# Seven block products for the last tile's second layer, and its weight sums on other engines

## The chip, the cores and the metric

The kernel runs on one core of a Trainium2 chip. The core has five engines that run at the same time and meet only through semaphores: TensorE (PE, matrix products), VectorE (DVE), ScalarE (ACT), GpSimd (POOL) and SyncE (SP, which issues transfers). Matrix products end in PSUM, a memory of eight banks of 128 x 512 fp32; everything else lies in SBUF. PE, DVE and ACT reach PSUM, GpSimd only SBUF.

The metric is the device time of one execution in microseconds (us). The kernel before took a median of 279.95 us in three runs (279.79 to 280.09).

## The reference

A linear attention is followed by a two-layer network. Cut to what is computed:

```python
# q, k, v: (8 batches, 8 heads, 576 rows, 64)
q_s = softmax(q, over the 64)
k_s = softmax(k, over the 576 rows)
kv  = einsum('bhsd,bhse->bhde', k_s, v)
x   = einsum('bhsd,bhde->bhse', q_s, kv)   # becomes 4608 tokens x 512
h   = x @ w_in                             # 512 x 2048
g   = maximum(0.01 * h, h)
out = g @ w_out                            # 2048 x 512
```

## The kernel before

The 4608 tokens are cut into nine tiles of 512 (`NT`, `TT`). A tile's first layer (`layer1`, L562) is 16 blocks j of 128 features, each the sum of four matmuls of 512 columns in bf16; ACT applies the leaky function (`leaky`, L572) and writes bf16 blocks g. The second layer (`layer2`, L584) makes for each of four groups of 128 tokens the sum of 16 matmuls; `store` (L577) copies the bank to SBUF and issues two transfers on SP's queue.

The attention of batch b is spread over the tiles before the one that needs it. The order of all work is written out by hand: `at(t, u, ...)` hangs functions on the point (tile t, step u), and `run(t, u)` calls them when the emission gets there. Steps 0 to 15 are the blocks of the first layer, 16 to 31 quarters of the token groups of the second. Each engine runs its own instructions strictly in the order of emission. `attend` (L486) writes the product of q and kv for some rows into banks, `x_keep` (L495) copies it into x's transposed store `xT`. For the last batch `at(6, 15)` (L817) attends seven of nine rows (`R7`, four banks) and then the last two (`RE`, two banks), the copies shared between ACT and DVE, and calls `token_sums`.

Banks come from two pools: `psB_pool` with six and `psO_pool` with two, the latter for the second layer's sums. The six buffers `raw_pool` hold the raw q, k, v of two batches, 9 KB per partition each, and serve other uses when the last batch has been read.

The last two tiles (TA = 7, TB = 8) do their first layer together, as a 2 x 2 product of blocks (tokens of tile 7 and 8; lower and upper half of the 512 inputs; lower and upper half of the 2048 features). It is done with seven block products in place of eight, by sums of blocks before and after. `weight_sums` (L791, at (6, 2)) makes t1 to t4 for all of w_in on DVE, four subtractions of 2048 elements, and GpSimd copies b22; the five results take five raw buffers. `token_sums` (L801) makes s1 to s4 on DVE and a22 on ACT. Sums and copies are fp32r, a 4-byte type for products. `pair_layer1` (L948) does one of eight row blocks i: seven products (`product`, L934) of two matmuls of 512 columns, with the additions on DVE (L958). Two products are plain bf16 (w_in by x), five are fp32r. Between the products PE does steps from `fill_steps`: the second layer of tile 6 that is left, then `pair_step` (L986), the second layer of tile 7. Tile 7's blocks lie in `g7`, tile 8's in `g8`, both where x of the tiles already used (`spent`) was.

Behind the eighth block PE finishes tile 7's second layer (L992), then does tile 8's (L1036): four groups of 16 matmuls of 512 columns, the last group cut at column 384 so that ACT and DVE copy its two parts.

The strip of code that orders the last attention and the sums:

```python
at(6, 2, weight_sums)
at(6, 15, lambda: attend_all(B - 1, (R7, (nc.scalar, nc.vector)), (RE, (nc.scalar, nc.vector))), token_sums)
```

Of the kernel before, what the change touches and what calls it, by code (L numbers as in the profile page):

```python
# [20 lines left out]
L = 64  # L21
# [5 lines left out]
def kernel(  # L27
# [499 lines left out]
    def attend_rows(b, rows, engs=(nc.scalar, nc.scalar)):  # L527
        groups = ((0, 1),) if rows.stop - rows.start <= 4 else ((0,), (1,))
        for ggs in groups:
            attend(b, ggs, rows)  # L530
# [253 lines left out]

    def plain(n):
# [5 lines left out]
    def weight_sums():  # L791
        w = lambda cs, fh: w_in_sb[:, cs, fh * (F // 2) : (fh + 1) * (F // 2)]
        for n in ("t1", "t3", "t2", "t4", "b22"):
            late[n] = raw_pool.tile([P, 2, R * HL * D // 2], F32R, name=n, tag="raw")[:, :, 0 : F // 2]
        subtract(nc.vector, "t1", w(CL, 1), w(CL, 0))
        subtract(nc.vector, "t2", w(CR, 1), plain("t1"))
        subtract(nc.vector, "t3", w(CR, 1), w(CL, 1))
        subtract(nc.vector, "t4", w(CR, 0), plain("t2"))
        nc.gpsimd.tensor_copy(out=late["b22"], in_=w(CR, 1))

    def token_sums():  # L801
        front.close()
        pool = ctx.enter_context(tc.tile_pool(name="late", bufs=1, reuse_waits="tile"))
        late["pool"] = ctx.enter_context(tc.tile_pool(name="late2", bufs=2, reuse_waits="tile"))
        both = raw_pool.tile([P, 2, R * HL * D // 2], F32R, name="s13", tag="raw")
        for i, n in enumerate(("s1", "s3")):
            late[n] = both[:, i, 0 : 2 * TT].rearrange("p (c n) -> p c n", c=2)
        for n in ("s2", "s4", "a22"):
# [97 lines left out]
    def layer2_at(t, g, tsub):  # L906
        po = psO_pool.tile([P, O], FP32, name="pout", tag="pout")
# [8 lines left out]
    for t in range(1, TA):  # L916
# [8 lines left out]
        for tsub in range(NTS if t < TA - 1 else 1):  # L925
            for _ in layer2_at(t, g_sb, tsub):
# [148 lines left out]
```

## Time and profile before

| | us |
|---|---|
| median of three runs | 279.95 |
| the profiled execution | 280.43 |
| its span, first to last instruction | 278.6 |
| TensorE busy | 270.6 |
| VectorE busy | 213.0 |
| ScalarE busy | 162.5 |
| GpSimd busy | 51.7 |

The times in the profile count from the start of the span. A row of the timeline reads: start, length, engine, line of the kernel, operation, output and inputs by name, shapes, how many instructions are merged into it, and in brackets how long the engine was idle before and what ended that. A row of the groups by form reads: line, engine, operation, names, shape and count, then busy us and mean ns of one, then idle time before. `PEld` is PE's weight load, which can run beside a matmul. The length of one matmul's record is longer than the time until the next can start, since matmuls are pipelined; the pace is read from many of them. A few matmul records can be missing from a trace.

### The profile page before, as it was taken

What the parts mean: (1) busy time and instruction counts of PE and PEld (TensorE: products, weight loads), DVE (VectorE), ACT (ScalarE), POOL (GpSimd) and SP (SyncE); (2) the same over time, 40 slices, a digit from 0 to 9 for tenths busy, and PEclk for the clock granted to TensorE, in tenths of its full rate; (3) what the DMA queues carried; (4) which work ended last, traced back from release to release, by engine and by line L of the source; (5) the groups of instructions that cost most, each with busy time, mean ns of one, the idle gap of its engine ahead of it and who ended that gap; (6) DMA issues with size and microseconds to landing.
All of it is one profiled execution on the core that took longest, in us unless ns stands there. A gap on an engine that the chain in (4) does not pass through costs nothing.

```text
span 278.6 us, 4917 instructions
## 1 busy us (share of the span) xinstructions
PE 270.6 (97%) x1912; PEld 135.7 (49%) x1938; DVE 213.0 (76%) x299; ACT 162.5 (58%) x285; POOL 51.7 (19%) x56
## 2 busy tenths in 40 slices
PE   8799999999999999999999999999999999999994
PEld 3378644444444444444444544454445555554443
DVE  2996985999999949966885597978959999891321
ACT  3977573783488367755586448664673757652000
POOL 2867450259003003000400070020000000000000
PEclk9999999999999999999999999999999999999999
DMA  6999999995994697099309930330601011100183
GB/s 236 341 208 324 242 255 309 396 307 160 287 406 167 91 395 262 2 251 397 100 0 269 390 86 2 85 76 1 161 0 40 0 38 40 38 1 0 43 185 75
DMA packets 40007, 46.46 MB, mean 167 GB/s; under 512 B 18736, under 2 KB 23344, under 8 KB 39984
## 3 DMA queue, kind: packets, MB, share of 16 engines
q1 hardware_dynamic: 36320, 41.82, 48.3%
q0 software_dynamic: 3504, 4.20, 8.7%
q8 instruction: 15, 0.25, 0.3%
q10 hardware_dynamic: 160, 0.13, 0.1%
q14 instruction: 8, 0.07, 0.1%
HBM read 36.70 MB, written 9.44 MB: 166 GB/s over the span
## 4 chain that ended last, share of the span: by engine, by line
PE 92%; DVE 3%; DMA 2%; issue 1%; ACT 0%; SPq 0%
PE pout L585 35%; PE ph L564 35%; PE pp L937 9%; PE pout L992 5%; PE pout L1036 5%; DMA k_raw<-in_k_dram 2%; PE po L478 1%; DVE t L159 1%; PE pokv L340 1%; PE pkv L340 1%; PE pkv L418 0%; DVE k_raw L409 0%; DVE e L958 0%; ACT ke L205 0%; DVE kmax L159 0%
## 5 line engine op out<-in xcount | busy, mean ns | idle before, releaser
L585 PE MATMUL pout<-w_out_sb,gj 128*128 128x512 bf16 x432 | 104.7, 380 | 1.1 <-issue 0.5
L564 PE MATMUL ph<-xT,w_in_sb 128*128 128x512 bf16 (+1 forms) x505 | 98.3, 352 | 0.4
L573 ACT ACTIVATE gj<-ph 128x512 bf16<-128x512 f32 x112 | 63.5, 602 | 19.1 <-PE ph L564 18.1
L564 PEld LDWEIGHTS <-w_in_sb 128*128 128x128 bf16 x512 | 49.8, 98 | 47.0 <-issue 0.2
L585 PEld LDWEIGHTS <-gj 128*128 128x128 bf16 x448 | 42.5, 98 | 54.9 <-issue 8.1
L579 ACT COPY out_sb<-pout 128x512 f32<-128x512 f32 (+1 forms) x25 | 14.5, 579 | 56.2 <-PE pout L1036 21.8
L217 POOL CAST vb<-v_raw 128x1152 bf16<-128x1152 f32 x13 | 21.4, 1680 | 82.7 <-DMA v_raw<-in_v_dram 82.7
L320 DVE TENSOR_REDUCE qsum<-qe 128x36 f32<-128x2304 bf16 (+5 forms) x13 | 20.0, 1542 | 6.9 <-ACT qe L311 6.7
L205 ACT ACTIVATE ke<-k_raw 128x2304 bf16<-128x2304 f32 (+2 forms) x13 | 18.0, 1383 | 7.9 <-DVE k_raw L197 7.7
L958 DVE TENSOR_TENSOR u<-pp,u 128x512 f32<-128x512 f32 x32 | 20.9, 685 | 1.8 <-PE pout L585 0.5
L327 DVE TENSOR_TENSOR qe<-qe,qrec 128x2304 bf16<-128x2304 bf16 (+5 forms) x13 | 21.5, 1657 | 0.5
L579 DVE COPY out_sb<-pout 128x512 f32<-128x512 f32 (+1 forms) x12 | 7.3, 652 | 18.8 <-PE pout L992 8.8
L244 DVE TENSOR_REDUCE qmax<-q_raw 128x36 f32<-128x2304 f32 (+5 forms) x13 | 19.9, 1536 | 0.0
L311 ACT ACTIVATE qe<-q_raw 128x2304 bf16<-128x2304 f32 (+5 forms) x13 | 17.2, 1321 | 3.7 <-POOL q_raw L303 2.8
L937 PE MATMUL pp<-s,t 128*128 128x512 f32 x48 | 18.6, 489 | 0.0
L197 DVE TENSOR_TENSOR k_raw<-k_raw,kall 128x1152 f32<-128x1152 f32 (+2 forms) x10 | 18.0, 1820 | 0.3
L303 POOL TENSOR_TENSOR q_raw<-q_raw,qmax 128x512 f32<-128x512 f32 (+3 forms) x7 | 11.8, 1682 | 20.5 <-DVE qmax L244 19.4
L303 DVE TENSOR_TENSOR q_raw<-q_raw,qmax 128x2304 f32<-128x2304 f32 (+1 forms) x6 | 14.7, 2448 | 0.2
L159 DVE TENSOR_TENSOR t<-t 128x256 f32<-128x256 f32 (+2 forms) x22 | 14.0, 636 | 0.7
L1036 PE MATMUL pout<-w_out_sb,xT 128*128 128x512 bf16 (+2 forms) x79 | 14.0, 336 | 0.1
L501 ACT CAST xT<-po 128x448 bf16<-128x448 f32 (+3 forms) x31 | 13.3, 513 | 1.1 <-PE po L478 1.1
L360 DVE RECIPROCAL krec<-pokv 128x2 f32<-128x2 f32 x8 | 1.3, 163 | 15.3 <-PE pokv L478 15.3
(100 smaller groups left out, 262.1 us busy)
## 6 DMA issues: line engine op xcount, KB each, us to landing
out_dram<-out_sb SPq DMA_DIRECT2D x70, 128.0 KB, 3.4
q_raw<-in_q_dram SPq DMA_DIRECT2D x6, 1152.0 KB, 9.3
v_raw<-in_v_dram SPq DMA_DIRECT2D x6, 1152.0 KB, 12.0
k_raw<-in_k_dram SPq DMA_DIRECT2D x5, 1152.0 KB, 7.3
k_raw<-in_k_dram SPq DMA_DIRECT2D x6, 576.0 KB, 5.7
v_raw<-in_v_dram SPq DMA_DIRECT2D x4, 576.0 KB, 7.7
w_in_sb<-in_moe_w_in_dram POOLq DMA_DIRECT2D x7, 256.0 KB, 6.8
w_out_sb<-in_moe_w_out_dram POOLq DMA_DIRECT2D x6, 256.0 KB, 9.2
```

What stands on the lines that cost most here:

```text
L217: eng.tensor_copy(out=o, in_=i)
L244: nc.vector.tensor_reduce(out=o, in_=st[b]["q"][:, hs, rs], axis=AX.X, op=ALU.max)
L303: eng.tensor_tensor(out=qs, in0=qs, in1=st[b]["qmax", rs.start, hs.start].unsqueeze(3).to_broadcast([P, m, n, D]), op=ALU.subtract,)
L320: nc.vector.reduce_sum(out=qsum, in_=q_cols(b, rs, hs), axis=AX.X)
L327: nc.vector.tensor_tensor(out=qes if out is None else out, in0=qes, in1=st[b]["qrec", rs.start, hs.start].unsqueeze(3).to_broadcast([P, n, ...
L564: nc.tensor.matmul(ph, lhsT=w_in_sb[:, cb, j * P : (j + 1) * P], rhs=xT[:, cb, c0 : c0 + n], start=(cb == 0 and first), stop=(cb == NB - 1 ...
L573: nc.scalar.activation(out=o, in_=ph, func=AF.Prelu, alpha=LEAKY_SLOPE)
L579: copy(out=out_sb, in_=pout)
L585: nc.tensor.matmul(pout, lhsT=g_sb[j // 2][:, j % 2, tsub * P : (tsub + 1) * P], rhs=w_out_sb[:, j, os], start=(j == 0), stop=(j == NF - 1),)
L937: nc.tensor.matmul(ps, lhsT=w(c)[:, i * P : (i + 1) * P], rhs=a(c), start=(c == 0), stop=(c == 1))
L958: nc.vector.tensor_tensor(out=o, in0=ps, in1=e, op=ALU.add)
L1036: nc.tensor.matmul(po, lhsT=g8(j)[:, tsub * P : (tsub + 1) * P], rhs=w_out_sb[:, j, os], start=(j == 0), stop=(j == NF - 1),)
```

## The change

Second layer of tile 8: the product of g (tokens by 2048 features) and w_out (2048 by 512) is now done with seven block products too. Its blocks are the two halves of the 512 tokens, of the 2048 features and of the 512 outputs. `product2` does one: 2 x 8 matmuls of 128 tokens by 256 columns, so 112 matmuls of 256 columns in all. Two products are plain bf16 (32 matmuls), five take fp32r sums (80). `out_weight_sums` makes v1 to v4 from w_out on DVE at (6, 2), and GpSimd copies o22. The sums of g (r1 to r4 on DVE, c22 on ACT) are made behind the last block of the pair stage, in memory that the pair stage's pools give back (`pairs.close()`). The partial results are added on DVE; the first and last output blocks are stored as soon as they are there, one half of each group issued by SP and one by ACT. Tile 7's stores copy on ACT.

w_in's sums: `in_weight_sums(i)` makes t1 to t4 for one row block, four subtractions of 256 elements on GpSimd, into one strip with room for two blocks; blocks 0 and 1 at (5, 26), block i + 2 behind block i. b22 is copied by block too (`last_weights`). In block 0 a copy of c22's first column on GpSimd stands ahead of the sums of block 2.

The last batch's two rows attend into the two banks of `psO_pool`; the first group of tile 6's second layer takes a bank of `psB_pool` instead. u2 and c22 have one buffer each instead of two, s1 and s3 their own tiles.

```diff
-    def attend(b, ggs, rows):
+    def attend(b, ggs, rows, pool=psB_pool, tag=BANK_TAG):
         n = (rows.stop - rows.start) * L
-        ps = [
-            psB_pool.tile([P, len(ggs), n], FP32, name="po", tag=BANK_TAG) for _ in range(2)
-        ]
+        ps = [pool.tile([P, len(ggs), n], FP32, name="po", tag=tag) for _ in range(2)]
...
-    def weight_sums():
-        w = lambda cs, fh: w_in_sb[:, cs, fh * (F // 2) : (fh + 1) * (F // 2)]
...
+    def out_weight_tiles():
+        for n in ("v1", "v3", "v2", "v4", "o22"):
+            late[n] = strip(n).rearrange("p a b -> p (a b)")[:, 0 : NH * H2].rearrange("p (m o) -> p m o", o=H2)
+
+    def out_weight_sums():
+        w = lambda fh, os: w_out_sb[:, fh * NH : (fh + 1) * NH, os]
+        subtract(nc.vector, "v1", w(0, E2), w(0, E1))
+        subtract(nc.vector, "v2", w(1, E2), plain("v1"))
+        subtract(nc.vector, "v3", w(1, E2), w(0, E2))
+        subtract(nc.vector, "v4", w(1, E1), plain("v2"))
+        nc.gpsimd.tensor_copy(out=late["o22"], in_=w(1, E2))
+
+    def in_weight_sums(i):
+        w = lambda cs, fh: w_in_sb[:, cs, (fh * NH + i) * P : (fh * NH + i + 1) * P]
+        if i == 0:
+            late["t"] = strip("t")
+        for n, k in zip(("t1", "t2", "t3", "t4"), range(4)):
+            late[n, i] = late["t"][:, k, i % 2 * 256 : i % 2 * 256 + 256].rearrange("p (c f) -> p c f", c=2)
+        for n, x, y in (
+            ("t1", w(CL, 1), w(CL, 0)),
+            ("t2", w(CR, 1), plain(("t1", i))),
+            ("t3", w(CR, 1), w(CL, 1)),
+            ("t4", w(CR, 0), plain(("t2", i))),
+        ):
+            subtract(nc.gpsimd, (n, i), x, y)
+        if i > 1:
+            last_weights(i)
+
+    def last_weights(i):
+        late["b22", i] = late["pool"].tile([P, 2, P], F32R, name="b22")
+        nc.gpsimd.tensor_copy(out=late["b22", i], in_=w_in_sb[:, CR, (NH + i) * P : (NH + i + 1) * P])
...
-    at(6, 2, weight_sums)
-    at(6, 15, lambda: attend_all(B - 1, (R7, (nc.scalar, nc.vector)), (RE, (nc.scalar, nc.vector))), token_sums)
+        last_weights(0)
+        last_weights(1)
+
+    at(5, 26, out_weight_tiles, lambda: in_weight_sums(0), lambda: in_weight_sums(1))
+    at(6, 2, out_weight_sums)
+    both = (nc.scalar, nc.vector)
+    at(6, 15, lambda: attend_all(B - 1, (R7, both), (RE, both, psO_pool, "pout")), token_sums)
...
-            for _ in layer2_at(t, g_sb, tsub):
+            for _ in layer2_at(t, g_sb, tsub, *((psB_pool, BANK_TAG) if t == TA - 1 else ())):
...
         add(c22, p5, u3)
+        if i == 0:
+            nc.gpsimd.tensor_copy(out=gate, in_=c22[:, 0:1])
...
+        if i + 2 < NH:
+            in_weight_sums(i + 2)
...
+    for first in (True, False):
+        for b in range(2):
...
+            if first:
+                nc.scalar.copy(out=o("c22"), in_=a22)
+                nc.vector.tensor_tensor(out=o("r1"), in0=a21, in1=a22, op=ALU.add)
+                nc.vector.tensor_tensor(out=o("r2"), in0=part("r1"), in1=a11, op=ALU.subtract)
+            else:
+                nc.vector.tensor_tensor(out=o("r3"), in0=a11, in1=a21, op=ALU.subtract)
+                nc.vector.tensor_tensor(out=o("r4"), in0=a12, in1=part("r2"), op=ALU.subtract)
...
-        store(TA * TT + tsub * P, pouts[tsub])
-    for tsub in range(NTS):
-        row0 = TB * TT + tsub * P
...
+        store(TA * TT + tsub * P, pouts[tsub], nc.scalar.copy)
+
+    def product2(a, w, each=False):
+        if each:
+            ps = [psB_pool.tile([P, H2], FP32, name="pq", tag=BANK_TAG) for _ in range(2)]
+        else:
+            both = psB_pool.tile([P, 2, H2], FP32, name="pq", tag=BANK_TAG)
+            ps = [both[:, 0], both[:, 1]]
+        for i in range(2):
+            for m in range(NH):
+                nc.tensor.matmul(
+                    ps[i],
+                    lhsT=a(m)[:, i * P : (i + 1) * P],
+                    rhs=w(m),
...
+    nc.scalar.copy(out=e1, in_=product2(plain_g(0), plain_w(0)))
+    ps = product2(plain_g(1), plain_w(1))
+    for i in range(2):
+        add(out1[i][:, E1], ps[:, i], e1[:, i])
+        put(out1[i], 0, i, E1)
+    add(u2, product2(rows("r2"), rows("v2")), e1)
+    add(u3, product2(rows("r3"), rows("v3")), u2)
+    ps = product2(rows("r1"), rows("v1"))
+    for i in range(2):
+        add(out2[i][:, E2], ps[:, i], u3[:, i])
+    add(u4, ps, u2)
+    ps = product2(rows("c22"), rows("v4"))
+    for i in range(2):
+        add(out2[i][:, E1], ps[:, i], u3[:, i])
+        put(out2[i], 1, i, slice(0, O))
+    ps = product2(rows("r4"), rows("o22"), True)
+    for i in range(2):
+        add(out1[i][:, E2], ps[i], u4[:, i])
+        put(out1[i], 0, i, E2)
```

More of the change, by code (lines that the diff above doesn't have):

```diff
@@ L789, in subtract @@
         eng.tensor_tensor(out=late[o], in0=a, in1=b, op=ALU.subtract)
-    def weight_sums():
-        w = lambda cs, fh: w_in_sb[:, cs, fh * (F // 2) : (fh + 1) * (F // 2)]
[L793 to L799, printed above, removed]
+    H2, M2 = O // 2, TT // 2
@@ L904, with layer2_at @@
         store(tsub * P, pout[tsub])
[L906 to L907 removed]
+    def layer2_at(t, g, tsub, pool=psO_pool, tag="pout"):
+        po = pool.tile([P, O], FP32, name="pout", tag=tag)
         for j in range(NF):
@@ L949, in pair_layer1 @@
         e1 = firsts[i]
-        u2, u3, u4, c22 = (late["pool"].tile([P, TT], FP32, name=n) for n in ("u2", "u3", "u4", "c22"))
+        u2, c22 = (late["one"].tile([P, TT], FP32, name=n) for n in ("u2", "c22"))
+        u3, u4 = (late["pool"].tile([P, TT], FP32, name=n) for n in ("u3", "u4"))
         if i < 2:
@@ new lines, in add, with put @@
+    def add(o, ps, e):
+        nc.vector.tensor_tensor(out=o, in0=ps, in1=e, op=ALU.add)
+    rows = lambda n: (lambda m: late[n][:, m])
+    plain_g = lambda fh: (lambda m: g8(fh * NH + m)[:, 0:M2])
+    plain_w = lambda fh: (lambda m: w_out_sb[:, fh * NH + m, E1])
+    out1, out2 = ([osb_pool.tile([P, O], FP32, name="out_sb") for _ in range(2)] for _ in range(2))
+    e1, u2, u3, u4 = (g_pool.tile([P, 2, H2], FP32, name="gu", tag="gj") for _ in range(4))
+    def put(o, half, i, cols):
+        for n, issue in enumerate((nc.sync, nc.scalar)):
+            b, c = divmod(TB * TT + half * M2 + i * P + n * L, S)
+            issue.dma_start(out=out_r[b, c // L, :, cols], in_=o[n * L : (n + 1) * L, cols])
```

61 lines of the change are left out of this document (31 added, 30 removed).

## The prediction

> **What bounds the kernel now.** I read the page first: busy time by engine and the shares of the chain that ended last.
>
> ```profile
> PE 270.6 (97%) x1912; PEld 135.7 (49%) x1938; DVE 213.0 (76%) x299; ACT 162.5 (58%) x285; POOL 51.7 (19%) x56
> ...
> PE 92%; DVE 3%; DMA 2%; issue 1%; ACT 0%; SPq 0%
> ```
>
> TensorE (PE) is busy for 97% of the span and makes up 92% of the chain, so an edit pays only by taking PE time away or by closing a PE wait, and costs as soon as it opens one. Next I cut the end of the run by its stages: the pair stage (first layer of the last two tiles by seven products, L937), the rest of the second layer of tile 7 (L992), the second layer of tile 8 (L1036), and the tail.
>
> ```profile
> 211.10:250.18 39.08, 38.89 (x170) 20.99 (x172) 36.31 (x56) 24.19 (x41) 0.00 (x0) 1.00 0.12 28
> 250.18:260.98 10.80, 10.75 (x50) 4.88 (x51) 1.86 (x4) 1.86 (x3) 0.00 (x0) 1.00 0.00 0
> 260.98:274.84 13.86, 13.81 (x80) 7.15 (x79) 4.12 (x7) 0.48 (x1) 0.00 (x0) 1.00 0.58 134
> 274.84:278.64 3.80, 0.16 (x3) 0.00 (x0) 0.29 (x1) 0.00 (x0) 0.00 (x0) 1.00 0.25 69
> ```
>
> The columns are length, then PE, PE weight loads, DVE, ACT and POOL busy, clock, DMA share, GB/s. PE is full in the first three at clock 1.00. The third, 13.86 us, is what the new code replaces. DVE is 93% busy in the pair stage and nearly idle in the 10.80 us behind it; GpSimd (POOL) does nothing from 211 on.
>
> **Part 1, the seven products of layer 2.** The 64 matmuls of L1036 go; 112 of 256 columns come: 32 in bf16 and 80 in fp32r. Their pace comes from these rows of the timeline and of the groups by form.
>
> ```profile
> 22.38 8.80 PE L564 MATMUL ph<-xT,w_in_sb 128*128 128x256 bf16 x79
> ...
> L564 PE MATMUL ph<-xT,w_in_sb 128*128 128x256 bf16 x128 | 14.8, 273 | 0.0
> ...
> 207.44 3.40 PE L585 MATMUL pout<-w_out_sb,gj 128*128 128x512 bf16 x15 [0.16 <-issue]
> ...
> 248.10 0.39 PE L992 MATMUL pout<-w_out_sb,gj 128*128 128x512 bf16 x1
> 248.15 0.81 PE L937 MATMUL pp<-s,t 128*128 128x512 f32 x2
> 248.80 0.39 PE L992 MATMUL pout<-w_out_sb,gj 128*128 128x512 bf16 x1
> ...
> 249.49 0.39 PE L992 MATMUL pout<-w_out_sb,gj 128*128 128x512 bf16 x1
> ```
>
> 79 bf16 matmuls of 256 columns took 8.80 us, the last one 0.27 from start to end, so the pace is (8.80 - 0.27) / 78 = 0.109 us. The same working on the 15 of 512 columns gives (3.40 - 0.38) / 14 = 0.216. From 248.10 to 249.49 run two bf16 matmuls and four fp32r ones, all of 512 columns: (1.39 - 2 x 0.216) / 4 = 0.240 for an fp32r one, 0.024 more than bf16. No row has fp32r at 256 columns. If the extra goes with the columns it takes 0.120; if it is fixed per matmul, 0.109 + 0.024 = 0.133. I take 0.122, near the first, since the bf16 rows at 256 and 512 columns are in proportion. The sum: 32 x 0.109 + 80 x 0.122 = 3.5 + 9.8 = 13.3 us against 13.86, a gain of 0.6; the ends are 0.8 gained and 0.3 lost. One eighth fewer columns is mostly eaten by the dearer type.
>
> The operand sums: eight DVE operations of 1024 elements (r1 to r4) and two ACT casts, issued behind the last block. The DVE rows for that size are the token sums (1.22 us, the row from 209.54 below): 8 x 1.22 = 9.8 us, in the 10.80 us in which DVE now does 1.86. The first four (r1, r2) are wanted only 3.5 us after that stretch, so this costs nothing; without the cover it would be up to 9.8. The four stores of tile 7 move from DVE to ACT, which is idle there. w_out's sums take the place of w_in's on DVE, four of 2048 elements for four of 2048: zero.
>
> The output buffers are four, so the first new outputs wait until tile 7's stores, eight issues on SP's queue, have landed; DVE's fifth copy does so now:
>
> ```profile
> 265.22 0.69 DVE L579 COPY out_sb<-pout 128x512 f32<-128x512 f32 x1 [2.20 <-DMA out_dram<-out_sb]
> ```
>
> DVE's later additions queue behind that wait of some 2 us, but PE has six banks for products of nearly 2 us each and goes on: zero, or about 1 us if the banks run out.
>
> The tail:
>
> ```profile
> L327 DVE TENSOR_TENSOR qe<-qe,qrec 128x256 bf16<-128x256 bf16 x1 | 0.4, 424 | 0.0
> ...
> L579 DVE COPY out_sb<-pout 128x128 f32<-128x128 f32 x1 | 0.3, 292 | 2.8 <-PE pout L1036 2.8
> ...
> out_dram<-out_sb ACTq DMA_DIRECT2D x1, 96.0 KB, 2.4
> ...
> out_dram<-out_sb ACTq DMA_DIRECT2D x1, 32.0 KB, 2.1
> ```
>
> The last operation grows from 128 to 256 columns, 0.424 - 0.292 = 0.13 us; the last transfer from 32 to 64 KB, by the two DMA rows half of 0.3, 0.15. The two output halves put six issues on ACT's queue and as many on SP's; ACT has no other work by then. Cost 0.28 us, between 0.1 and 0.6 if the 512 KB stored in the last 2 us queue up.
>
> **Part 2, the last two rows in the output pool's banks.** The chain at this place:
>
> ```profile
> 206.34 0.61 ACT gj L573
> ...
> 206.99 0.30 PE po L478 x6
> ...
> 206.44 0.41 PE L478 MATMUL po<-qX,kd 64*64 64x448 bf16 x6
> ```
>
> The crosses of the first seven rows run four at a time; their second group starts at 206.44 and takes 448/512 x 0.216 = 0.19, to 206.63. The crosses of the other two rows wait for the bank that ACT frees at 206.95 and go on at 206.99. With banks of their own they follow at 206.63: 0.35 us gained (bounds 0 and the 0.55 from 206.44). What is late next is below.
>
> **Part 3, w_in's sums on GpSimd.** This is where the cost can lie. The rows show how POOL and DVE stand to each other, and what DVE does before the pair stage:
>
> ```profile
> 181.39 1.90 POOL L799 CAST b<-w_in_sb 128x2048 fp32r<-128x2048 bf16 x1 [15.75 <-ACT ke L205]
> ...
> 181.66 4.03 DVE L303 TENSOR_TENSOR q_raw<-q_raw,qmax 128x2304 f32<-128x2304 f32 x1
> ...
> 159.99 2.56 DVE L303 TENSOR_TENSOR q_raw<-q_raw,qmax 128x2304 f32<-128x2304 f32 x1
> ...
> 36.70 2.25 POOL L197 TENSOR_TENSOR k_raw<-k_raw,kall 128x576 f32<-128x576 f32 x1
> ...
> 37.75 1.08 DVE L320 TENSOR_REDUCE qsum<-qe 128x14 f32<-128x896 bf16 x1
> ...
> 35.10 1.08 DVE L320 TENSOR_REDUCE qsum<-qe 128x14 f32<-128x896 bf16 x1
> ...
> L303 POOL TENSOR_TENSOR q_raw<-q_raw,qmax 128x512 f32<-128x512 f32 x3 | 3.1, 1041 | 15.3 <-DVE qmax L244 14.8 <-DVE krec L429 0.5
> ...
> L303 POOL TENSOR_TENSOR q_raw<-q_raw,qmax 128x768 f32<-128x768 f32 x1 | 1.5, 1477 | 3.4 <-DVE qmax L244 3.4
> ...
> 187.07 2.19 ACT L311 ACTIVATE qe<-q_raw 128x2304 bf16<-128x2304 f32 x1
> ...
> 192.30 2.56 DVE L327 TENSOR_TENSOR qe<-qe,qrec 128x2304 bf16<-128x2304 bf16 x1
> 194.77 2.29 DVE L789 TENSOR_TENSOR t<-w_in_sb 128x2048 fp32r<-128x2048 bf16 x1
> ...
> 201.51 2.28 DVE L789 TENSOR_TENSOR t<-w_in_sb,t 128x2048 fp32r<-128x2048 bf16 x1
> 206.69 1.49 DVE L503 CAST xT<-po 128x448 bf16<-128x448 f32 x3 [2.90 <-PE po L478]
> ...
> 209.54 1.22 DVE L789 TENSOR_TENSOR s<-s,xT 128x1024 fp32r<-128x1024 f32 x1
> ...
> 211.14 0.82 PE L937 MATMUL pp<-s,t 128*128 128x512 f32 x2
> ```
>
> The DVE subtraction of 2304 elements took 4.03 us when a POOL cast had begun before it, and 2.56 without: it stood until the cast ended at 183.29. A DVE operation with one SBUF operand (the sums of L320) takes 1.08 beside a POOL operation or not. The Trainium skill's page "SBUF — State Buffer", section "SBUF: two separate sides", gives the rule: GpSimd and a DVE operation with two SBUF inputs hold a shared port pair as an exclusive lock, for the whole instruction. By that rule, the trace agrees (4.03 against 2.56).
>
> A GpSimd sum of 256 elements, by the rows of 512 and 768, takes 1041 - (1477 - 1041) = 605 ns. Eight of them come at (5, 26), then w_out's copy (2048 elements, 1.90 as now). The strip for the sums is the last raw buffer given out, so it waits for batch 7's q, read until 187.07 + 2.19 = 189.26. By 192.30 some five are done; then DVE has two-operand work without a pause until 201.51 + 2.28 = 203.79. Three sums and the copy, 3 x 0.605 + 1.90 = 3.7 us, push in between. DVE's free time before 206.69 is 2.90, so x's eviction and the token sums behind it, queued on DVE, start up to 0.8 late; if six are done, 0.5. I take 0.65 (bounds: 0 if nothing collides, 8 x 0.605 + 1.90 - 2.90 = 3.8 if all do).
>
> Who waits: PE's first pair product wants s2, which is ready at 209.54 + 1.22 = 210.76 and used at 211.14. That is 0.38 of slack, of which Part 2 takes 0.35. So PE enters the pair stage at 0.65 - 0.38 = 0.27 later than now: the gain of Part 2 is gone (ends: 0.35 earlier, 3.4 later).
>
> In the stage itself POOL owes four sums and a copy per block, 4 x 0.605 + 0.24 (1.90 x 256/2048) = 2.7 us of a block's 39.08 / 8 = 4.9, a block ahead; the products of block n free the strip's half for n + 2. The copy that holds POOL until block 0's c22 is there delays the sums of block 2 alone, which have a block's time left. The copies of b22 for blocks 0 and 1, 0.24 each, come while DVE evicts from banks. Cost nothing, if the additions of DVE, which read one bank and one SBUF operand, run beside POOL as the 1.08 rows do. The POOL cast at 181.39 is gone there, which gives DVE 1.5 us ahead of an ACT operation that starts at 187.07 anyway: nothing.
>
> **The sum.** +0.27 (pair stage begins later) - 0.6 (products) + 0.28 (tail) = -0.05 us. The profiled execution took 280.43 us (span 278.6 and 1.8 around it), 0.48 above the median of 279.95. I predict 280.4 for a run like it, and 279.9 for the median: no change that can be measured. (What a measurement can tell from none is about 0.2%, 0.56 us.)
>
> **Rivals.**
> - A, faster: nothing collides before 206.69 and fp32r goes at 0.120: -0.35 - 0.8 + 0.28 = -0.87, 279.1 us. For it: 2.90 us of DVE slack. Chance 0.27.
> - B, slower by the lock: more of the eight sums are left at 192.30. At 2 us of lateness the sum is 2 - 0.38 - 0.6 + 0.28 = +1.3, 281.2; with all in the way +3.1, 283.0. It decides from 1.3 us of lateness. Against it: three idle microseconds before 192.30. Chance 0.14.
> - C, fixed extra: 0.133 per fp32r matmul: 0.27 + 0.3 + 0.28 = +0.85, 280.8. For it: only 512 columns have been seen. Chance 0.13.
> - D, weight loads set the pace. A load of fp32 weights lasts 0.19 and the matmul only 0.12:
>
> ```profile
> L937 PEld LDWEIGHTS pp<-s,t 128*128 128x128 f32 x48 | 9.3, 194 | 1.7
> ...
> 9.72 0.19 PEld L372 LDWEIGHTS pout<-zero 128*128 128x128 f32 x1 [0.17 <-issue]
> ...
> 9.72 0.30 PEld L372 LDWEIGHTS pout<-zero 128*128 128x128 f32 x2 [0.17 <-issue]
> ...
> L1036 PEld LDWEIGHTS <-xT 128*128 128x128 bf16 x80 | 7.2, 98 | 6.9
> ```
>
>   At 0.20 per matmul the 80 take 16.0 instead of 9.8, 286.1 us with the other terms. Against it: two loads of 0.19 ended 0.30 after the first began, so the second began 0.11 in; at 0.11 they hide. The Trainium skill's page "TensorE: Matmul & The Clock Gate", section "Weight-path perf modes", says that fast weight load is off for FP32; by that rule, the trace agrees (0.19 against 0.098 for bf16), and it leaves D a chance. Chance 0.06.
> - E, GpSimd in the pair stage holds DVE's additions or comes late: 2.7 us a block in six blocks less DVE's 39.08 - 36.31 = 2.8 of spare time, +13, some 293. Against it: the 1.08 rows. Chance 0.03.
>
> **How the numbers follow.** My forecast, -0.5 to +0.5, has 0.37. Faster 0.27 (A), same 0.37, slower 0.36 (B, C, D, E). The likeliest case's own range is 279.4 to 280.5. The range of 8 in 10 is 278.9 to 281.8: below it lies the part of A with both best ends at once, above it D, E and half of B.
>
> **What would show it.** Right: 32 matmuls at 0.109 and 80 near 0.12 with no gaps; the crosses at 206.6; POOL's sums from 189.3, the last stretched by DVE; DVE subtractions over 2.5 us; a PE wait below 1 us before the first fp32r product; then the pair stage 39.1 long. Wrong: fp32r pairs at 0.13 or 0.20, PE waiting on GpSimd inside the pair stage, additions over 0.7 us beside POOL, or a last transfer landing later than 2.6 us after its issue.

## The result and the profile after

The kernel after takes a median of 279.39 us (279.17 to 279.73, 20 runs); the kernel before, run beside it, 280.02 us (279.79 to 280.29, 20 runs). The ratio is 0.9975 with a 95% interval of 0.9967 to 0.9984: faster by 0.25%, 0.63 us, which is just beyond what can be told from no change. The prediction was 279.9 us, range 278.9 to 281.8, and gave "faster" 0.27. The profiled execution took 279.63 us against 280.43.

The page of after, its busy times and the shares of its chain:

```profile
PE 270.2 (97%) x1945; PEld 141.4 (51%) x1970; DVE 223.0 (80%) x310; ACT 166.2 (60%) x291; POOL 76.4 (28%) x97
...
PE 93%; DVE 3%; DMA 2%; issue 1%; ACT 0%; SPq 0%; ACTq 0%
```

PE is still the bound. DVE is busy for 10 us more and GpSimd for 25 us more, yet DVE's share of the chain is 3% as before and GpSimd has none.

Two profiles are compared from a common mark, because they differ by some tenths before it: the start of the last activation (`gj`) of tile 6's first layer, the last that is done plainly, at 206.34 in before. These are the rows of the timeline of after around it and behind it, and the chain:

```profile
206.04 0.69 PE L478 MATMUL po<-qX,kd 64*64 64x448 bf16 x16
206.14 0.60 ACT L571 ACTIVATE gj<-ph 128x512 bf16<-128x512 f32 x1 [0.21 <-PE ph L562]
...
206.50 1.49 DVE L501 CAST xT<-po 128x448 bf16<-128x448 f32 x3 [2.85 <-PE po L478]
...
210.72 0.70 PE L967 MATMUL pp<-s,t 128*128 128x512 f32 x2
...
260.42 3.66 PE L1091 MATMUL pq<-w_out_sb,xT 128*128 128x256 bf16 x32
...
271.58 2.08 PE L1091 MATMUL pq<-o,r 128*128 128x256 f32 x16
...
273.70 0.42 DVE L1101 TENSOR_TENSOR out_sb<-pq,gu 128x256 f32<-128x256 f32 x1 [0.53 <-PE pq L1091]
```

```profile
202.87 3.24 PE ph L562 x15
206.11 0.61 PE po L478 x16
```

All 16 crosses of the last batch now run as one row; in before six of them came behind the activation, at 206.99. The first two fp32r matmuls end at 210.72 + 0.70 = 211.42, 5.28 us behind the mark; in before at 211.14 + 0.82 = 211.96, 5.62 behind it. PE enters the pair stage 0.34 us earlier.

The stages, cut at the same places as in the prediction; the first cut lies 0.34 us nearer to the mark than in before, by the ends just read (length, PE, weight loads, DVE, ACT, POOL, clock, DMA share, GB/s):

```profile
206.14:210.56 4.42, 4.37 (x34) 2.05 (x34) 3.92 (x6) 3.02 (x6) 0.00 (x0) 1.00 0.00 0
210.56:249.64 39.08, 38.89 (x171) 20.95 (x173) 36.63 (x57) 23.93 (x41) 17.86 (x31) 1.00 0.12 28
249.64:260.42 10.78, 10.73 (x51) 4.89 (x51) 10.61 (x11) 4.30 (x6) 0.00 (x0) 1.00 0.01 2
260.42:273.50 13.08, 13.08 (x113) 12.69 (x111) 4.81 (x11) 2.19 (x5) 0.00 (x0) 1.00 0.42 102
273.50:277.80 4.30, 0.16 (x2) 0.00 (x0) 0.42 (x1) 0.00 (x0) 0.00 (x0) 0.85 0.58 176
```

The pair stage and the rest behind it take what they took (39.08 + 10.78 against 39.08 + 10.80), although GpSimd now works in the one and DVE fills the other. The products take 13.08 us instead of 13.86. The tail is 0.5 us longer.

For the table, two lengths are read from each profile: from the mark to the end of the last matmul (in after 271.58 + 2.08 = 273.66, less 206.14), and from there to the end of the span. Each kernel ran beside runs of the kernel before, so it is the ratios that compare. One run of e_psB, its profiled one, ran at a granted clock of 0.66 and took 403.1 us; the ratio and the median leave it out, and the lengths are those of e_psB_again.

| kernel | median us | ratio to before, 95% | mark to last matmul | behind it | sum |
|---|---|---|---|---|---|
| before | 280.02 | | 68.67 | 3.64 | 72.31 |
| after | 279.39 | 0.9975 (0.9967 to 0.9984) | 67.52 | 4.16 | 71.68 |
| e_psB, e_psB_again | 279.85 | 0.9990 (0.9981 to 0.9999) | 67.89 | 4.08 | 71.97 |
| e_eight | 279.83 | 0.9997 (0.9987 to 1.0007) | 68.32 | 3.63 | 71.95 |
| e_strip | 279.59 | 0.9980 (0.9971 to 0.9989) | 67.52 | 4.15 | 71.66 |
| e_late | 279.52 | 0.9976 (0.9966 to 0.9986) | 67.55 | 4.14 | 71.69 |
| e_dve | 286.22 | 1.0217 (1.0203 to 1.0231) | 74.17 | 4.20 | 78.36 |
| e_bf16 | 279.02 | 0.9956 (0.9943 to 0.9970) | 66.70 | 4.33 | 71.03 |
| e_tail | 285.06 | 1.0177 (1.0163 to 1.0191) | 67.54 | 9.61 | 77.14 |
| e_tail2 | 279.46 | 0.9974 (0.9964 to 0.9984) | 67.51 | 4.03 | 71.54 |
| e_spread | 279.34 | 0.9971 (0.9959 to 0.9983) | 67.55 | 4.02 | 71.57 |
| e_best | 278.82 | 0.9952 (0.9940 to 0.9965) | 66.70 | 4.17 | 70.87 |

The change by this table: 1.15 us less up to the last matmul, 0.52 more behind it, 0.63 less in all, as the medians say. The lengths come from one profiled execution of each kernel; where a kernel's end was left as it is, the length behind the last matmul lies between 4.08 and 4.20.

### The profile page after: what moved, and what is told of

It is laid out like the page before. It is cut to its first block, busy times and chain, and to the rows that moved or that the text cites. A ratio compares the mean times of both kernels' runs of the same rounds, so it can differ in the third digit from the quotient of the medians.

```text
span 277.8 us, 5089 instructions
## 1 busy us (share of the span) xinstructions
PE 270.2 (97%) x1945; PEld 141.4 (51%) x1970; DVE 223.0 (80%) x310; ACT 166.2 (60%) x291; POOL 76.4 (28%) x97
## 3 DMA queue, kind: packets, MB, share of 16 engines
HBM read 36.70 MB, written 9.44 MB: 166 GB/s over the span
## 4 chain that ended last, share of the span: by engine, by line
PE 93%; DVE 3%; DMA 2%; issue 1%; ACT 0%; SPq 0%; ACTq 0%
PE pout L583 35%; PE ph L562 35%; PE pp L967 9%; PE pout L1027 5%; PE pq L1091 5%; DMA k_raw<-in_k_dram 2%; PE po L478 2%; DVE t L159 1%; PE pokv L340 1%; PE pkv L340 1%; PE pkv L418 0%; DVE k_raw L409 0%; ACT ke L205 0%; DVE kmax L159 0%; ACT e L976 0%
## 5 line engine op out<-in xcount | busy, mean ns | idle before, releaser
L577 ACT COPY out_sb<-pout 128x512 f32<-128x512 f32 x28 | 16.0, 585 | 39.0 <-PE pout L583 20.4
L303 DVE TENSOR_TENSOR q_raw<-q_raw,qmax 128x2304 f32<-128x2304 f32 (+1 forms) x6 | 13.2, 2202 | 0.2
L789 POOL TENSOR_TENSOR t<-w_in_sb 128x256 fp32r<-128x256 bf16 x16 | 11.4, 712 | 7.1 <-PE pp L967 7.1
L159 DVE TENSOR_TENSOR t<-k_raw 128x512 f32<-128x512 f32 (+1 forms) x11 | 12.1, 1102 | 1.2 <-DMA k_raw<-in_k_dram 1.0
```

What stands on the lines that cost most here:

```text
L159: nc.vector.tensor_tensor(out=o, in0=i0, in1=i1, op=ALU.max)
L303: eng.tensor_tensor(out=qs, in0=qs, in1=st[b]["qmax", rs.start, hs.start].unsqueeze(3).to_broadcast([P, m, n, D]), op=ALU.subtract,)
```

## The experiments

The theory after the comparison: Part 2 gives 0.34 us, Part 1 gives 0.78 and takes 0.52 back in the tail, Part 3 costs nothing. The rivals: that one of these gains is made up of something else, that GpSimd's sums cost time that another gain hides, and that the tail has another cause. Each kernel is the kernel after with one edit.

### Part 2 undone (e_psB, e_psB_again)

```diff
-    at(6, 15, lambda: attend_all(B - 1, (R7, both), (RE, both, psO_pool, "pout")), token_sums)
+    at(6, 15, lambda: attend_all(B - 1, (R7, both), (RE, both)), token_sums)
-            for _ in layer2_at(t, g_sb, tsub, *((psB_pool, BANK_TAG) if t == TA - 1 else ())):
+            for _ in layer2_at(t, g_sb, tsub, *()):
```

> The kernel after, with Part 2 alone undone: the last two rows of batch 7 attend in psB again and tile 6's second layer takes psO. Theory (Part 2 is on PE's path): the crosses of RE wait for the two banks that R7's outputs hold, as in the kernel before, PE comes into the pair stage about 0.34 us later and keeps that to the end, since nothing between there and the last matmul can take it up: about 279.7 us, a ratio to the kernel before near 0.9989. Rival (the 0.34 us is given back, because DVE's v's and s's end late anyway and the first pair product waits for them): the same time as the kernel after, 279.4 us, ratio 0.9975.

> The kernel after with Part 2 alone undone, once more, for its profile. Theory: ScalarE's and VectorE's eviction of R7's outputs ends before the crosses of RE begin, the crosses of R7 and RE have a gap of about 0.35 us between them, and the first fp32r product of the pair stage starts 0.34 us later, counted from the last activation ahead of the attention, than in the kernel after (4.65 us after it). Rival: no gap, or the same start of the first fp32r product.

The rows come from e_psB_again. Its timeline and its chain:

```profile
206.03 0.60 ACT L571 ACTIVATE gj<-ph 128x512 bf16<-128x512 f32 x1 [0.21 <-PE ph L562]
...
210.83 0.81 PE L967 MATMUL pp<-s,t 128*128 128x512 f32 x2
```

```profile
206.03 0.61 ACT gj L571
...
206.68 0.30 PE po L478 x6
```

The six crosses stand behind the activation again, and the first two fp32r matmuls end at 210.83 + 0.81 - 206.03 = 5.61 behind the mark, against 5.28: 0.33 us. By its start alone the pair is only 0.22 later (4.80 against 4.58), less than the 0.34 expected. A matmul's record can begin while the one before it runs, so the ends tell the pace. Up to the last matmul the loss is 0.37 us, by the ratios 0.4 (0.9990, where 0.9989 had been expected). The theory holds; the rival, that the gain is given back, falls.

### Part 1 undone (e_eight)

```diff
-    at(6, 2, out_weight_sums)
...
-    nc.scalar.copy(out=e1, in_=product2(plain_g(0), plain_w(0)))
...
+    for tsub in range(NTS):
...
+            for j in range(NF):
...
+                    lhsT=g8(j)[:, tsub * P : (tsub + 1) * P],
+                    rhs=w_out_sb[:, j, os],
```

> The kernel after, with Part 1 alone undone: the last tile's second layer by the eight products of the kernel before (DVE stores the first 128 rows, the last 128 in two pieces); the sums of w_out and of the hidden units that only Part 1 needs are gone with it. Theory: the products last 13.85 us instead of 13.08 (+0.77), the work behind the last matmul 3.80 instead of 4.30 us (-0.5), and nothing ahead of them changes, since PE waits for none of the removed sums: +0.27 us, 279.7 us, ratio 0.9985. Rival (the removed DVE sums in the four products ahead and the four in the stage before had held PE up): below that, 279.1 to 279.4 us, ratio 0.997 or less.

```profile
260.09 14.02 PE L1071 MATMUL pout<-w_out_sb,xT 128*128 128x512 bf16 x80
...
274.14 0.29 DVE L577 COPY out_sb<-pout 128x128 f32<-128x128 f32 x1 [2.80 <-PE pout L1071]
```

The eight products take 14.02 us by their row; the seven take 260.42 to 273.66, 13.24. Up to the last matmul the table gives +0.80, behind it -0.53, together +0.27, which was the number expected. The medians say +0.4, the ratios 0.6, with an uncertainty that just takes in 0.27. That DVE's removed sums had held PE up is refuted: from the mark to the first of the products pass 54.30 us here (205.79 to 260.09) and 54.28 in after (206.14 to 260.42).

### The strip in another buffer (e_strip)

```diff
-        for n in ("v1", "v3", "v2", "v4", "o22"):
+        for n in ("v1", "v3", "v2", "v4", "t", "o22"):
```

> The kernel after with the order of two buffers exchanged: the strip of w_in's first-column sums gets the fifth free buffer, which batch 7's q holds until ScalarE has read it, and the copy o22 the sixth. So GpSimd's sums begin near 189 us and the o22 copy, 1.9 us, stands behind the first of them, which is what the prediction assumed. Nothing else is changed. Prediction's mechanism (sums and copy of GpSimd overlap DVE's two-operand work of 192 to 204 us and hold it up): DVE's subtractions of that stretch last 2.5 us and more instead of 2.28, the last s ends 0.5 to 0.9 us later, PE enters the pair stage later by 0.3 to 0.6 us than in the kernel after, time 279.7 to 280.0 us, ratio 0.9985 to 1.000. Rival (GpSimd at 0.67 us a row takes no time from DVE, or DVE's slack covers it): subtractions still 2.28 us, the same time as the kernel after, 279.4 us.

The edit did not do what it was to do. The rows of GpSimd in the kernel after show where the sums and the copy run, and they run there in e_strip as well (first sum at 164.02, copy at 189.15):

```profile
165.41 1.10 POOL L789 TENSOR_TENSOR t<-w_in_sb 128x256 fp32r<-128x256 bf16 x1
...
170.74 0.67 POOL L789 TENSOR_TENSOR t<-w_in_sb,t 128x256 fp32r<-128x256 bf16 x1
189.13 1.89 POOL L807 CAST o<-w_out_sb 128x2048 fp32r<-128x2048 bf16 x1 [17.72 <-ACT qe L311]
```

The sums begin at 165.4 behind GpSimd's cast of v, 24 us before the prediction had them, and it is the copy o22 that waits for batch 7's q. In the compiled program the strip lies at one address in both kernels, in the buffer of batch 5's q. Buffers go out in the order in which they are first written, not in which they are named, and the strip is written first. The next kernel, e_late, bears this out: there the strip is written last, and it waits for ACT's read of batch 7's q. So the run of e_strip repeats the kernel after, and its time (0.9980) does too.

### The collision made (e_late)

```diff
-    at(5, 26, out_weight_tiles, lambda: in_weight_sums(0), lambda: in_weight_sums(1))
-    at(6, 2, out_weight_sums)
+    at(5, 26, out_weight_tiles)
+    at(6, 2, out_weight_sums, lambda: in_weight_sums(0), lambda: in_weight_sums(1), lambda: out_copy(slice(1, NH)))
```

`out_copy(ms)` copies the blocks ms of o22; `out_weight_sums` now copies block 0 only.

> The kernel after with the collision made that the prediction feared: the first eight sums of w_in are issued behind w_out's, with the strip in the buffer of batch 7's q, and of the copy o22 one eighth goes ahead of them and seven eighths behind. The computation is the same. GpSimd's sums then begin at 189.3 us and need 8 x 0.67 + 1.7 = 7.1 us, to 196.4 without hindrance, while DVE has two-operand work from 192.1 to 203.65. Prediction's mechanism (GpSimd's and DVE's two-operand work exclude each other, and each pushes the other back): 7.1 - 2.8 = 4.2 us of GpSimd's work fall into DVE's row of such operations, DVE's multiplication and subtractions last up to 4.2 us longer in all, x's eviction and the sums of tokens are late by 4.2 - 2.85 = 1.3 us, and PE enters the pair stage about 1.3 us later: 280.7 us, ratio 1.002. Rival (a GpSimd sum of 256 elements holds DVE up for little or nothing, or DVE's idle 2.85 us cover it all): the time of the kernel after, 279.4 us, ratio 0.9975.

GpSimd and DVE in the timeline of e_late:

```profile
188.84 0.67 POOL L789 TENSOR_TENSOR t<-w_in_sb 128x256 fp32r<-128x256 bf16 x1 [7.56 <-ACT qe L311]
...
192.22 2.87 POOL L789 TENSOR_TENSOR t<-w_in_sb,t 128x256 fp32r<-128x256 bf16 x1
...
200.40 3.74 POOL L810 CAST o<-w_out_sb 128x1792 fp32r<-128x1792 bf16 x1
```

```profile
191.79 2.77 DVE L327 TENSOR_TENSOR qe<-qe,qrec 128x2304 bf16<-128x2304 bf16 x1
194.49 2.76 DVE L789 TENSOR_TENSOR v<-w_out_sb 128x2048 fp32r<-128x2048 bf16 x1
197.28 2.64 DVE L789 TENSOR_TENSOR v<-w_out_sb,v 128x2048 fp32r<-128x2048 bf16 x1
199.84 2.76 DVE L789 TENSOR_TENSOR v<-w_out_sb 128x2048 fp32r<-128x2048 bf16 x1
202.52 3.76 DVE L789 TENSOR_TENSOR v<-w_out_sb,v 128x2048 fp32r<-128x2048 bf16 x1
206.20 1.47 DVE L501 CAST xT<-po 128x448 bf16<-128x448 f32 x3
```

The same engine in after:

```profile
194.58 2.28 DVE L789 TENSOR_TENSOR v<-w_out_sb 128x2048 fp32r<-128x2048 bf16 x1
```

This is the picture that the prediction drew: four sums of 0.67 us are done before DVE's multiplication begins at 191.79, a fifth ends inside it, and then the two engines take turns. A sum that needs 0.67 us stands 2.7 to 2.9 us, over a whole DVE operation, and the copy is pushed into the last subtraction. DVE's five rows come to 14.69 us; in after they are 2.56, 2.28, 2.29, 2.28 and 2.29, 11.70. So the end of the fifth sum, three more sums and the copy cost DVE 2.99 us. The mechanism is shown. But DVE's idle time ahead of x's eviction was 2.85 us, and the eviction begins 0.37 behind the mark, against 0.36 in after: the whole collision went into the idle time and the kernel's time did not move (0.9976). It used that time up: the eviction's row shows no idle time ahead of it any more. What a longer collision would do no run shows. The 4.2 us expected here were too many: three sums lengthened a DVE row by 0.35 to 0.48 us each, not 0.67, and the copy by 1.47, not 1.7. The rival's second half, the cover, decides.

### The block sums on DVE (e_dve)

```diff
-            subtract(nc.gpsimd, (n, i), x, y)
+            subtract(nc.vector if i > 1 else nc.gpsimd, (n, i), x, y)
```

> The kernel after with w_in's sums of blocks 2 to 7 (24 operations of 256 elements, inside the pair stage) on DVE instead of GpSimd; GpSimd keeps the first eight and the copies. Theory (DVE is full in the pair stage, 36.4 of 39.0 us, so the sums per block can only be had on GpSimd): 24 x 0.29 to 0.42 us = 6.8 to 10.2 us more on DVE against 2.6 us of spare time, so PE waits 4 to 7.6 us, 283.5 to 287 us, ratio 1.012 to 1.025. Rival (the spare time and the 10.4 us behind the stage take them up, since DVE may run late by some banks): less than 1 us, below 280.4 us.

The groups of e_dve by form, and its pair stage:

```profile
L967 PE MATMUL pp<-s,b 128*128 128x512 f32 x16 | 6.1, 461 | 2.8 <-DVE u L989 2.8
...
L789 DVE TENSOR_TENSOR t<-w_in_sb,t 128x256 fp32r<-128x256 bf16 x12 | 5.1, 422 | 0.3
...
L789 DVE TENSOR_TENSOR t<-w_in_sb 128x256 fp32r<-128x256 bf16 x12 | 5.0, 417 | 0.0
```

```profile
211.00:250.00 39.00, 34.62 (x142) 17.07 (x145) 37.47 (x69) 19.32 (x35) 2.54 (x7) 1.00 0.12 27
```

The 24 sums cost DVE 10.1 us, PE waits for DVE's additions and comes to its last matmul 6.65 us later, inside the 4 to 7.6 us of the theory; 6.8 by the ratio. The remaining 3.45 us went into DVE's spare time. So DVE had room for a third of them, and the sums are free only because they run elsewhere. That they are free on GpSimd the timeline of after shows, GpSimd and DVE in one stretch:

```profile
217.62 0.68 POOL L789 TENSOR_TENSOR t<-w_in_sb 128x256 fp32r<-128x256 bf16 x1
218.26 0.68 POOL L789 TENSOR_TENSOR t<-w_in_sb,t 128x256 fp32r<-128x256 bf16 x1
```

```profile
217.35 0.68 DVE L989 TENSOR_TENSOR u<-pp,e 128x512 f32<-128x512 f32 x1
218.13 0.69 DVE L989 TENSOR_TENSOR e<-pp,e 128x512 f32<-128x512 f32 x1
```

Neither is lengthened: a sum takes 0.67 at 170.74, with no two-operand work on DVE beside it, and an addition 0.69 at 212.76, before GpSimd starts. An addition reads one bank and one SBUF operand. The Trainium skill's page "SBUF — State Buffer", section "SBUF: two separate sides", says that the lock takes in a DVE operation when it has two SBUF inputs and the GpSimd operation reads SBUF, or when it runs in a two-port mode; by that rule, the trace agrees on both sides (2.28 to 2.76 us in e_late, 0.68 unchanged here).

### bf16 sums for the last products (e_bf16)

```diff
-    for n in ("r1", "r2", "r3", "r4", "c22"):
-        late[n] = pool.tile([P, NH, M2], F32R, name=n)
+    for n in ("r1", "r2", "r3", "r4"):
+        late[n] = pool.tile([P, NH, M2], BF16, name=n)
...
-        nc.gpsimd.tensor_copy(out=late["o22"], in_=w(1, E2))
+        late["o22"] = w(1, E2)
```

> The kernel after with the operand sums of the last seven products (v1 to v4 and r1 to r4) rounded to bf16 instead of fp32r, and o22 and c22 read from w_out and from the hidden units as they are, without copies: the computation differs in that rounding. Theory (a matmul of 256 columns costs 0.120 us in fp32r and 0.109 in bf16, and nothing else paces the products): the 80 matmuls take 80 x 0.011 = 0.88 us less, the products end 0.88 us earlier and with them the kernel: 278.5 us, ratio 0.9945. Rival (something else than the type paces the products, as DVE's additions or the banks): 279.2 to 279.4 us, with gaps between the products.

The groups by form, two of after and one of e_bf16:

```profile
L1091 PE MATMUL pq<-v,r 128*128 128x256 f32 x48 | 6.0, 284 | 0.0
...
L1091 PEld LDWEIGHTS pq<-v,r 128*128 128x128 f32 x48 | 5.8, 191 | 0.0
```

```profile
L1090 PE MATMUL pq<-v,r 128*128 128x256 bf16 x48 | 5.4, 273 | 0.0
```

48 matmuls take 5.4 us in place of 6.0: (5.4 - 0.27) / 47 = 0.109 against (6.0 - 0.28) / 47 = 0.122 from these rounded rows. Up to the last matmul the kernel gains 0.82 us of 0.88 expected. The type is what paces these products. Of the gain 0.17 is lost again behind the last matmul, and by the medians and ratios 0.4 to 0.5 us are left (279.02, where 278.5 had been expected).

### The tail (e_tail, e_tail2, e_spread)

The last two outputs by one DMA each (e_tail):

```diff
+            one.dma_start(out=out_r[b, c // L : c // L + 2, :, cols], in_=o[:, cols])
-        put(out1[i], 0, i, E2)
+        put(out1[i], 0, i, E2, (nc.scalar, nc.sync)[i])
```

Both halves of the last output but one on SP's queue (e_tail2):

```diff
-        put(out1[i], 0, i, E2)
+        put(out1[i], 0, i, E2, ((nc.sync, nc.sync), (nc.scalar, nc.sync))[i])
```

The second half of the output stored in two steps (e_spread):

```diff
         add(out2[i][:, E2], ps[:, i], u3[:, i])
+        put(out2[i], 1, i, E2)
...
-        put(out2[i], 1, i, slice(0, O))
+        put(out2[i], 1, i, E1)
```

> The kernel after, with the last two outputs (second columns of the tile's first half) each written by one DMA instead of two: the first by ScalarE's queue alone, the second by SyncE's alone. The bytes are the same. Theory (the span's end hangs on the last issue, which ScalarE gives 0.24 us after SyncE's because it is still issuing its half of the output before): the last issue comes about 0.24 us earlier, and the end with it: 0.2 us less, 279.2 us, ratio to the kernel before 0.9967. Rival 1 (the end hangs on the bytes behind the last issue, 64 KB in one queue's descriptors instead of two times 32 KB): no change or 0.1 to 0.3 us more, 279.4 to 279.7 us.

> The kernel after with both halves of the last output but one on SyncE's queue, so that ScalarE's queue is free when the last addition ends; the last output stays split over both queues, and every DMA keeps its form of 64 rows of 1 KB. Theory (the end hangs on the last issue, and ScalarE's came 0.24 us late because it was still issuing): the last issue begins at about 274.2 instead of 274.385 in the profile's time, the end is 0.1 to 0.2 us earlier, 279.2 to 279.3 us. Rival (the end hangs on the bytes still in the queues): no change, 279.4 us, the last landing still near 276.8.

> The kernel after with the second half of the tile's output stored in two steps: its second columns as soon as the fifth product is added, 1.9 us before its first columns, instead of both together behind the sixth product. Four more DMAs, the same bytes. Theory (the tail of the kernel after is set by the bytes: 512 KB and 256 KB issued from 272.2 on keep the DMA engines full from 273.5 to 276.3): 256 KB move ahead of that, the engines are no longer full, and the end hangs on the last issue and its landing again, as in the kernel before: 0.3 to 0.6 us less, 278.8 to 279.1 us, ratio 0.9955 to 0.9965. Rival (the end hangs on the last issue, which is late as it is, and two more issues of 0.5 us on each queue push it back further): no change to 0.3 us more, 279.4 to 279.7 us.

A window of e_tail (the last two columns are the DMA engines' share and GB/s):

```profile
276.50:282.20 5.70, 0.00 (x0) 0.00 (x0) 0.00 (x0) 0.00 (x0) 0.00 (x0) 0.64 0.12 44
```

Neither theory nor rival foresaw 5.7 us more. The DMA of 128 rows has the two groups of 64 rows as its outer dimension; it runs at a share of 0.12, which is two of sixteen engines, at 44 GB/s. The run says nothing on the issue's lateness, since the form of the DMA changed more than was meant. The Trainium skill's page "DMA: Bandwidth & Descriptors", section "Why a DMA increments its semaphore by 16 and not by 1", says that a DMA is spread over the largest number of engines, up to 16, that divides the outermost dimension (of size above 1) of both sides; by that rule, two here, and the trace agrees (0.12).

The windows of after and then of e_spread behind the products:

```profile
273.50:274.50 1.00, 0.16 (x2) 0.00 (x0) 0.42 (x1) 0.00 (x0) 0.00 (x0) 1.00 1.00 299
274.50:275.50 1.00, 0.00 (x0) 0.00 (x0) 0.00 (x0) 0.00 (x0) 0.00 (x0) 1.00 0.84 258
275.50:276.30 0.80, 0.00 (x0) 0.00 (x0) 0.00 (x0) 0.00 (x0) 0.00 (x0) 1.00 0.81 251
```

```profile
273.50:274.50 1.00, 0.10 (x1) 0.00 (x0) 0.42 (x1) 0.00 (x0) 0.00 (x0) 1.00 0.81 211
274.50:275.50 1.00, 0.00 (x0) 0.00 (x0) 0.00 (x0) 0.00 (x0) 0.00 (x0) 1.00 0.77 197
275.50:276.30 0.80, 0.00 (x0) 0.00 (x0) 0.00 (x0) 0.00 (x0) 0.00 (x0) 1.00 0.37 96
```

In after the engines are busy at 0.81 to 1.00 until 276.3. In e_tail2 the last issue came not earlier but later (274.70 instead of 274.39, since SP's queue then held three issues of 0.55 us), and yet the tail became 0.13 us shorter, 4.03: so the last issue's time is not what sets the end, and the theory of that run falls. In e_spread the share falls to 0.37 in the last window and the tail is 4.02, a gain of 0.14 us where 0.3 to 0.6 were expected. It stores in pieces of 1 KB, which ran at 197 to 211 GB/s instead of 251 to 299. The kernels whose tail was left alone show 4.08 to 4.20, so both gains are little more than the scatter, and by the medians both kernels are as fast as the kernel after.

Where the 0.52 us lie can be read from the last store, which ACT issues in all of these kernels but e_tail2. The issues in before and then in after, and a table of the last one, from the trace's records of issues and landings:

```profile
273.78 1.22 PE L1036 MATMUL pout<-w_out_sb,xT 128*128 128x384 bf16 x17
...
274.70 1.39 ACTq L582 DMA_DIRECT2D out_dram<-out_sb  x2
```

```profile
264.63 10.31 ACTq L1112 DMA_DIRECT2D out_dram<-out_sb  x6
```

| kernel | last matmul to last issue | issue to landing | landing to the end of the span |
|---|---|---|---|
| before | 0.35 | 2.11 | 1.17 |
| after | 0.72 | 2.41 | 1.03 |
| e_tail2 | 1.06 | 2.01 | 0.97 |
| e_spread | 0.70 | 2.02 | 1.30 |
| e_bf16 | 0.89 | 2.39 | 1.05 |
| e_best | 0.88 | 2.02 | 1.27 |

From before to after the last issue begins 0.37 us later: 0.13 for the longer addition, and 0.24 because ACT is still issuing its half of the output before. The landing takes 0.30 longer, and behind it 0.14 come back. In the four other kernels whose tail was left alone and whose last products are in fp32r, the three columns lie at 0.71 to 0.72, 2.32 to 2.45 and 1.03 to 1.05, so these differences are clear of the scatter. With the issue 0.34 later still, e_tail2 lands no later (3.07 behind the last matmul against 3.13), while e_spread, with the issue where it was, lands 0.41 earlier: so in after the bytes under way set the last landing, as the theory of e_spread has it. But 0.27 of that is lost behind the landing. There SP waits for the stores one after the other (L1159 in after), a record every 0.06 us; 2 such records are left behind the last landing in e_tail2, 3 in after, 5 in before and 7 in e_spread, and the last column grows with them.

### Both together (e_best)

The edits of e_bf16 and e_spread in one kernel.

> The kernel after with two edits together: the operand sums of the last seven products in bf16 (which rounds them), and the output's second half stored in two steps. Theory (the bf16 products end 0.85 us earlier, of which 0.25 us were lost to full DMA engines at the end; the two-step store takes that away): 0.85 us and 0.3 to 0.6 us less than the kernel after, 278.0 to 278.3 us, ratio 0.9925 to 0.994. Rival (the two do not add up, since the end hangs on the last issues): as with the bf16 sums alone, 278.9 us, ratio 0.9956.

The time is 278.82 us, ratio 0.9952, 0.5 us above the nearer end of the theory (278.3) and close to the rival. Up to the last matmul the 0.82 us are there again. Behind it nothing is lost to the kernel after (4.17 against 4.16). The 0.17 that e_bf16 lost is its last issue, at 0.89 instead of 0.72 behind the last matmul; here the issue is as late (0.88), the landing is faster (2.02), and the waits behind it are longer (1.27). The kernel has the lowest median here, 0.6 us below the kernel after, with sums rounded to bf16; its ratio cannot be told from that of e_bf16 (0.9956).

## Why the prediction was right and wrong

The time came out inside the range, 0.5 us below the forecast, as rival A has it: "nothing collides" and "fp32r goes at 0.120", forecast there at 279.1. The likeliest case, no change that can be measured, did not come true. That the forecast's own number came within 0.5 us is in part luck: all three terms of its sum were off, the first by its sign too, and the tail took back a part of what the other two gained.

| term | predicted | measured | by |
|---|---|---|---|
| pair stage begins (Parts 2 and 3) | +0.27 | -0.34 | 5.28 against 5.62 behind the mark; e_psB_again, e_late |
| products (Part 1) | -0.6 | -0.78 | 13.24 against 14.02; e_eight |
| tail (Part 1) | +0.28 | +0.52 | 4.16 against 3.64; e_eight |
| sum | -0.05 | -0.60 | mark to the end of the span -0.63, medians -0.63 |

- **Part 2** was right: 0.35 worked out from the second group of crosses, 0.34 measured, and 0.33 when undone.
- **Part 3** is the step that failed, in the sentence that begins "The strip for the sums is the last raw buffer given out, so it waits for batch 7's q". It is the first that is written, and so it got the buffer that is free first. GpSimd made the eight sums at 165.4 to 171.4, and DVE's subtractions kept their 2.28 us. The second half of the step, the price, failed too, as e_late shows: with the collision there (and one eighth of the copy ahead of it), DVE lost 2.99 us where 3.7 had been worked out, and its idle time took nearly all of it. So the +0.65 was zero in both cases, and Part 2's gain was not eaten. The signs named for it, GpSimd's sums from 189.3 and subtractions over 2.5 us, did not appear in after. No run has Part 3 alone; that it costs nothing rests on the pair stage's length, on e_late, and on the other two parts, which make up 0.60 of the 0.63 us.
- **A GpSimd sum** takes 0.67 us by its rows, 0.605 had been taken, and the copy of 256 elements 0.40 in place of 0.24; without effect.
- **Part 1, pace.** "I take 0.122, near the first": it is (2.08 - 0.283) / 15 = 0.120 by the row of the last 16 (0.122 by the first 48), in proportion to the columns, and (3.66 - 0.273) / 31 = 0.109 in bf16. Rival C (0.133) and rival D (0.20) fall: the fp32 loads still show 0.19 each but follow one another every 0.12 us, beside the matmuls. The weight load does not become the bound.
- **Part 1, covers.** The sums of g lay in the 10.8 us behind the pair stage as said (DVE 10.61 of 10.78), the stores moved to ACT cost nothing, PE ran through the products without a gap (13.08 of 13.08), and DVE's wait for stores to land, some 2 us in the prediction, was 0.3.
- **The tail** was the mis-sized term: the longer addition was right (0.13), the rest was taken at 0.15 and is 0.39. That the last issue stands behind others in ACT's queue was put at nothing ("ACT has no other work by then") and is 0.24; the landing was taken at 0.15 and is 0.30; and 0.14 come back in the closing waits. The upper bound of 0.6 "if the 512 KB stored in the last 2 us queue up" held. The last transfer landed 2.41 us after its issue, below the 2.6 that had been named as a sign of being wrong.
- **Rival E** (GpSimd holding DVE in the pair stage) falls by the 0.68 us rows on both sides. The two 1.08 us rows that the prediction set against it both stand beside GpSimd operations (34.00 to 36.73 and 36.70 to 38.95), so they did not show "or not"; the additions at 212.76 and 217.35 show both.
- **Rival B** falls as far as e_late goes: the lock is real, but the collision it needs goes into DVE's idle time. A longer one was not tried, and e_late left no idle time that could cover it.

## What to carry to other kernels

An engine lock is priced in three steps: whether the two operations meet at all, which depends on which buffer is free first; how much one lengthens the other, less than the other's whole row; and what idle time lies behind. The largest term of this prediction died at the first step and would have died at the third. A gain in matmul columns is worth its type's pace (seven eighths of the columns, but 0.120 instead of 0.109 for five products in seven), and the end that comes with it has to be priced by the last issue's place in its queue, by all the bytes that become ready late and by the waits that close the program: the last operation and the last piece alone gave 0.28 of the 0.52 us.

## What the runs showed of the hardware

- GpSimd and DVE in two-operand work alternate operation by operation: a 0.67 us sum then shows 2.7 to 2.9 us, and lengthens a 2.28 us subtraction by only 0.35 to 0.48.
- fp32r matmuls cost 1.10 times bf16 ones at 256 columns (0.120, 0.109), and 1.11 times at 512 (0.240, 0.216).
- A store of 128 rows whose outer dimension is 2 used two of sixteen DMA engines, 44 GB/s; as two DMAs of 64 rows the same bytes left with the engines at 0.81 and more.
- Behind the last landing SP waits for the stores one after the other, a record every 0.06 us: with 2, 3, 5 and 7 of them left, the span ended 0.97, 1.03, 1.17 and 1.30 us after the landing.
- Sums written in bf16 instead of fp32r took DVE 0.69 us instead of 1.22 for 1024 elements (rows of e_bf16 and of after).
